# Decode attention with grouped queries: three zeroed tiles in one allocation with one memset, and the second and fourth K quarters of two tiles on shared semaphores

## Chip, cores and metric

One core of one Trainium2 chip. The metric is the device time of one execution in microseconds (us), lower is better. The record marks all executions told of here as fast, and all comparisons are between such runs. Engines: PE is TensorE (matmul), DVE is VectorE, ACT is ScalarE, POOL is GpSimd, SP is SyncE, which here only issues loads. "SPq" in a profile line is SP's instruction queue.

## Reference

```python
B, Hq, Hkv, Sq, Sk, D = 1, 32, 8, 1, 65536, 128      # all bf16
scores = einsum("bhqd,bhkd->bhqk", q, repeat(k, 4)) * D ** -0.5
out = einsum("bhqk,bhkd->bhqd", softmax(scores), repeat(v, 4))
```

K and V are 134 MB each and are read once. Each of the eight K/V heads serves four query rows.

## The kernel before

For each head g the keys are cut into two tiles (b = 0 and 1) of 32,768 keys, 8.39 MB each. SP issues the loads of K and V tiles in a fixed order into one big SBUF buffer with three slots: two for K, one for V.

```python
io = sb("io", [P, 3 * SL, D], bf16)        # three slots; SL = 256 rows of each partition
...
ex = sb("ex", [P, 4, 512], bf16)           # exponentials
et = sb("et", [P, 2, 512], bf16)
vs = sb("vs", [P, D + 2], fp32)            # sum of the value matmuls, and the two row sums
vy = sb("vy", [P, D, 4], fp32)
...
k_lo = [0, 64, 128, 192]
s_k = {(b, lo): sem(f"s_k{b}_{lo}") for b in range(2) for lo in k_lo}

def load_k(g, b):
    SP.wait((s_sc, 16 * g - 8 + 8 * b if g else 0))      # PE is done with the slot's old K
    cuts = k_lo + [SL] if (g, b) in ((0, 0), (G - 1, 1)) else [0, 128, SL] if g == 0 else [0, SL]
    for lo, hi in zip(cuts, cuts[1:]):
        load(k, g, b, 1 + b, s_k[b, lo], lo, hi)
...
load_k(0, 0)
load_k(0, 1)
for g in range(1, G):
    for b in range(2):
        load_k(g, b)
        load_v(g - 1, b)                                  # waits for PE to be done with the old V
```

DVE transposes each tile in four quarters, and before each it takes 16 from that quarter's semaphore. PE then computes scores in eight groups per tile and counts them in `s_sc`. The loop body is the same for every head, so all four quarters are always taken. But most tiles are loaded whole, and then only the first quarter's semaphore is paid by the load. The others are **prepaid**: POOL adds enough to them at a point where it can do no harm, and the later takes find the money there.

```python
def transposes(b, lo, hi):
    for t in range(lo, hi, 64):
        d_take(s_k[b, t], 16)                             # wait for 16, subtract 16
        part = io[:, (1 + b) * SL + t:(1 + b) * SL + t + 64, :]...
        dve.transpose(out=part, in_=part).then_inc(s_kt, 2)
```

POOL's start, before any of this, and DVE's:

```python
GP.mark(gp.memset(wz[:, :, :], 0.0))
GP.mark(gp.memset(vs[:, :], 0.0))
GP.mark(gp.memset(ex[:, :, :], 0.0))
GP.mark(gp.memset(vy[:, :, :], 0.0))
n = GP.mark(gp.memset(ident[:, :], 0.0))
GP.after(n)
p_ident = GP.mark(gp.affine_select(out=ident[:, :], ...))
...
for s in (s_k[1, 64], s_k[1, 192]):                       # prepaid from the start
    gp.sem_inc(s, 16 * (G - 1))
...
DV.mark(dve.memset(acc[:, :], 0.0))
DV.wait((s_gp, p_ident))
DV.mark(dve.tensor_reduce(out=sel[:, :], in_=ident..., op=ALU.add))
...                                                       # selq, sely, qT, y_sum, then the K transposes
```

## Time and profile before

| | before |
|---|---|
| median | 629.82 us (6 runs, 629.33 to 630.03) |
| span of the profiled execution | 627.7 us |
| busy: PE, DVE, ACT, POOL | 57%, 55%, 5%, 2% |
| transfers | 268.49 MB, mean 428 GB/s |

Three lines of the profile's page, before. The DMA row cuts the span into 40 slices; each digit is the busy share of the sixteen DMA engines in tenths.

```profile
PE   1865483827638275381844808458193571886346
DMA  8999999999999999999999999999999999999996
...
q1 hardware_dynamic: 6944, 268.45, 99.2%
```

PE comes and goes; the transfers never pause for a visible time. The queue that carries K and V fills 99.2% of the span.

The start, in the timeline of the kernel before. Columns: start in us, duration in us, engine, line, operation, output and input, count; in brackets, how long the engine had been idle and what released it.

```profile
1.52 0.21 POOL L187 MEMSET vs<- 128x130 f32 x1
1.67 1.81 POOL L188 MEMSET ex<- 128x2048 bf16 x1
3.41 0.52 POOL L189 MEMSET vy<- 128x512 f32 x1
...
4.65 0.38 DVE L208 TENSOR_REDUCE sel<-ident 128x4 f32<-128x128 f32 x1 [0.90 <-POOL ident L192]
...
8.50 4.45 DVE L373 STREAM_TRANSPOSE io<-io 128x4096 uint32<-128x4096 uint32 x1 [1.34 <-DVEq L119]
...
32.89 8.77 DVE L373 STREAM_TRANSPOSE io<-io 128x4096 uint32<-128x4096 uint32 x2 [5.11 <-DVEq L119]
```

DVE waits 0.90 us for POOL's identity. Later it waits again, 1.34 us, before its first K transpose, and there it waits for the first quarter of K to land, 7.4 us after its issue at 0.96 us (the release shows as DVE's own queue, in which the take of the load's semaphore stands). At 32.89 us the first half of K tile 1 has landed (issued at 2.97 us, 29.8 us to landing) and two quarters are transposed without a break.

The loads that SP issues next (timeline of SP, before):

```profile
33.28 0.43 SPq L137 DMA_DIRECT2D io<-in_v_dram  x1
57.31 0.33 SPq L137 DMA_DIRECT2D io<-in_k_dram  x1
95.12 0.33 SPq L137 DMA_DIRECT2D io<-in_v_dram  x1
```

And the end: three pieces of the chain of work that ended last, before (start, duration, what).

```profile
609.01 12.42 DMA io<-in_v_dram
...
622.53 1.80 PE pf L359 x28
...
624.89 0.36 ACT o L487
```

### The profile page before, as it was taken

The numbers are of one execution on the slowest core, as the hardware profiler recorded it, in microseconds if no ns is written. First come the engines' busy times: TensorE is split into PE (matmuls) and PEld (weight loads), VectorE is DVE, ScalarE is ACT, GpSimd is POOL, SyncE is SP. The second block draws the span as 40 slices with busy tenths as digits, with TensorE's granted clock in tenths as the row PEclk, the third lists the DMA queues.
The fourth block names the chain that finished last, engine by engine and source line by source line (L and its number), as shares of the span: only waits on it lengthen the run. The fifth ranks groups of instructions, "written<-read, shape, count | busy, mean of one in ns | idle before, by whom it ended". The sixth has DMA issues, their size and how long they took to land. (4 is left out here: it accounts for less than half of the span.)

```text
span 627.7 us, 7067 instructions
## 1 busy us (share of the span) xinstructions
PE 356.4 (57%) x2142; PEld 139.8 (22%) x2142; DVE 345.5 (55%) x154; ACT 34.4 (5%) x26; POOL 9.7 (2%) x42
## 2 busy tenths in 40 slices
PE   1865483827638275381844808458193571886346
PEld 0322131312213032130321303123031230332112
DVE  7795835649066490764807557084670946684210
ACT  0000100020000200002000020000200002000100
POOL 2000000000000000000000000000000000000000
PEclk9978595967959678596785958859587695899676
DMA  8999999999999999999999999999999999999996
GB/s 362 441 468 401 468 401 468 401 468 401 468 401 464 405 459 409 447 422 447 422 438 430 426 443 409 459 405 464 401 468 401 468 401 468 396 437 434 434 432 274
DMA packets 7003, 268.49 MB, mean 428 GB/s; under 512 B 856, under 2 KB 1112, under 8 KB 1496
## 3 DMA queue, kind: packets, MB, share of 16 engines
q1 hardware_dynamic: 6944, 268.45, 99.2%
q8 instruction: 1, 0.02, 0.0%
q14 instruction: 2, 0.02, 0.0%
q10 hardware_dynamic: 56, 0.01, 0.0%
HBM read 268.44 MB, written 0.01 MB: 428 GB/s over the span
## 5 line engine op out<-in xcount | busy, mean ns | idle before, releaser
L301 PE MATMUL acc<-io,wz 128*128 x1024 | 272.7, 420 | 184.8 <-PEq L119 157.3
L373 DVE STREAM_TRANSPOSE io<-io 128x4096 uint32<-128x4096 uint32 x64 | 279.9, 4416 | 157.2 <-DVEq L119 157.2
L301 PEld LDWEIGHTS acc<-io,wz 128*128 x1024 | 106.4, 104 | 351.2 <-issue 272.5
L254 PE MATMUL acc<-io,et 128*16 128x512 bf16 x1016 | 72.5, 416 | 19.3 <-PEq L119 19.2
L440 ACT ACTIVATE ex<-acc,nmb 128x2048 bf16<-128x2048 f32 x8 | 15.7, 1967 | 556.9 <-DVE nmb L420 556.9
L410 DVE TENSOR_REDUCE mg<-acc 128x1 f32<-128x2048 f32 x8 | 18.3, 2291 | 48.3 <-DVEq L119 48.3
L254 PEld LDWEIGHTS acc<-io,et 128*16 128x16 bf16 x1016 | 27.7, 94 | 58.4 <-issue 35.5
L248 PE MATMUL pf<-vs,sel 128*4 128x130 f32 (+1 forms) x20 | 5.7, 386 | 54.2 <-PEq L119 54.2
L376 DVE STREAM_TRANSPOSE et<-ex 128x1024 bf16<-128x1024 bf16 x17 | 20.8, 1225 | 22.6 <-SPq L154 12.8
L450 ACT ACTIVATE acc<-wz 128x2560 f32<-128x2560 bf16 (+2 forms) x8 | 16.3, 2040 | 1.0 <-ACT ex L440 0.2
L412 DVE TENSOR_REDUCE m<-pt 1x4 f32<-1x128 f32 x8 | 2.2, 279 | 22.7 <-DVEq L119 22.7
L514 POOL COPY wz<-qT 32x16 bf16<-32x16 bf16 x32 | 6.1, 189 | 512.6 <-PE acc L301 440.3
L248 PEld LDWEIGHTS pf<-vs,sel 128*4 128x4 f32 x20 | 1.2, 83 | 54.7 <-issue 54.6
L326 PE MATMUL pt<-et 128*16 128x512 bf16 x32 | 13.1, 411 | 0.0
L384 DVE TENSOR_REDUCE vs<-vy 128x128 f32<-128x512 f32 x9 | 6.1, 681 | 7.6 <-DVEq L119 7.6
L423 DVE TENSOR_TENSOR vy<-acc,sely 128x512 f32<-128x512 f32 x8 | 8.5, 1064 | 0.0
L472 DVE TENSOR_TENSOR vy<-acc,sely 128x512 f32<-128x512 f32 x1 | 0.7, 691 | 11.5 <-PE acc L254 11.5
L343 PE MATMUL pb<-ident,nrow 1*128 1x1 f32 x8 | 1.6, 194 | 7.5 <-PEq L119 7.5
L326 PEld LDWEIGHTS pt<-et 128*16 128x16 bf16 x32 | 3.1, 97 | 4.5 <-issue 1.4
L341 PE MATMUL pt<-ident,mg 128*1 128x128 f32 x8 | 2.3, 283 | 2.6 <-PEq L119 2.6
L420 DVE COPY nmb<-pb 128x1 f32<-128x1 f32 x8 | 1.3, 157 | 3.9 <-DVEq L119 3.9
L343 PEld LDWEIGHTS pb<-ident,nrow 1*128 1x128 f32 x8 | 1.1, 139 | 8.9 <-issue 8.9
(31 smaller groups left out, 22.8 us busy)
## 6 DMA issues: line engine op xcount, KB each, us to landing
io<-in_v_dram SPq DMA_DIRECT2D x5, 4096.0 KB, 16.9
io<-in_k_dram SPq DMA_DIRECT2D x8, 2048.0 KB, 27.4
io<-in_k_dram SPq DMA_DIRECT2D x2, 4096.0 KB, 34.4
io<-in_v_dram SPq DMA_DIRECT2D x1, 2048.0 KB, 10.3
io<-in_v_dram SPq DMA_DIRECT2D x1, 1024.0 KB, 12.4
io<-in_v_dram SPq DMA_DIRECT2D x3, 256.0 KB, 12.8
io<-in_v_dram SPq DMA_DIRECT2D x2, 128.0 KB, 12.8
io<-in_k_dram SPq DMA_DIRECT2D x13, 48.4
```

What stands on the lines that cost most here:

```text
L248: return pe.matmul(out=pf[0:H, 0:w], lhsT=sel[:, :], rhs=vs[:, 0:w], skip_group_check=True, **kw)
L254: return pe.matmul(out=vacc[32 * c:32 * c + 16, :, :], lhsT=et[:, ch // 2, w0:w0 + 16], rhs=io[:, PS * ch + 4 * tt:PS * ch + 4 * tt + 4, : ...
L301: i = pe.matmul(out=bass.AP(acc, r_o, [[2560, P], [1, 512]]), lhsT=bass.AP(wz, r_w + ((2 * s + e) * WB - 4 * u), [[4 * WB, P], [1, P]]), r ...
L326: pe.matmul(out=pt[0:16, :], lhsT=et[:, 0, 0:16], rhs=et[:, 0, :], start=True, stop=True)
L373: dve.transpose(out=part, in_=part).then_inc(s_kt, 2)
L376: dve.transpose(out=et[:, :, :].rearrange("p i n -> p (i n)"), in_=ex[:, 2 * b:2 * b + 2, :].rearrange("p i n -> p (i n)"),).then_inc(s_et, 1)
L384: DV.mark(dve.tensor_reduce(out=vs[:, 0:D], in_=vy[:, :, :], axis=AX.X, op=ALU.add))
L410: dve.tensor_reduce(out=mg[:, :], in_=sc, axis=AX.X, op=ALU.max).then_inc(s_mg, 1)
L423: dve.tensor_tensor(out=vy[:, :, :].rearrange("p d y -> p y d"), in0=vacc, in1=sely[:, :, None].to_broadcast([P, 4, D]), op=ALU.mult,).the ...
L440: act.activation(out=ex[:, :, :].rearrange("p b n -> p (b n)"), in_=sc, func=ACT.Exp, bias=nmb[:, :], scale=SCALE, accum_out=vs[:, D + g % ...
L450: act.activation(out=part, in_=wz[:, 0, 0:1].to_broadcast([P, part.shape[1]]), func=ACT.Copy).then_inc(s_cl, 1)
L514: gp.tensor_copy(out=wz[r, :, c0:c0 + H].rearrange("p (s w) h -> p s w h", s=2), in_=qTb[r, :, :, g, :],).then_inc(s_w, 1)
```

## The change

The intent: fewer POOL instructions and a shorter set-up, and two semaphores fewer in use. `ex`, `vy` and `vs` become views of one fp32 tile that one memset clears. For the second and fourth quarters, tile 1 now takes from tile 0's semaphore. Those can no longer be prepaid from the start, since tile 0's real quarters would be taken too early. POOL therefore waits for the eighth score group of tile 0 and pays fourteen takes then.

```diff
-    ex = sb("ex", [P, 4, 512], bf16)
     et = sb("et", [P, 2, 512], bf16)
-    vs = sb("vs", [P, D + 2], fp32)
-    vy = sb("vy", [P, D, 4], fp32)
+    zs = sb("zs", [P, 1024 + 4 * D + D + 2], fp32)
+    ex = zs[:, 0:1024].bitcast(bf16).rearrange("p (b n) -> p b n", n=512)
+    vy = zs[:, 1024:1024 + 4 * D].rearrange("p (d y) -> p d y", y=4)
+    vs = zs[:, 1024 + 4 * D:]
...
+    for lo in k_lo[1::2]:
+        s_k[1, lo] = s_k[0, lo]
...
-    GP.mark(gp.memset(vs[:, :], 0.0))
-    GP.mark(gp.memset(ex[:, :, :], 0.0))
-    GP.mark(gp.memset(vy[:, :, :], 0.0))
+    GP.mark(gp.memset(zs[:, :], 0.0))
...
-    for s in (s_k[1, 64], s_k[1, 192]):
-        gp.sem_inc(s, 16 * (G - 1))
...
+            if g == 1:
+                GP.wait((s_sc, 8))
+                for t in k_lo[1::2]:
+                    gp.sem_inc(s_k[0, t], 16 * (2 * G - 2))
             GP.wait((s_sc, 16 * g))
             gp.sem_inc(s_sd, 1)
             if g == 1:
-                for t in k_lo[1:]:
-                    gp.sem_inc(s_k[0, t], 16 * (G - 1))
+                gp.sem_inc(s_k[0, 128], 16 * (G - 1))
                 gp.sem_inc(s_k[1, 128], 16 * (G - 2))
```

## The prediction

> **What bounds the kernel now.** The transfers. The page's DMA row reads 9 tenths in all slices but the first and last; the queue table gives the K/V queue 99.2% of the sixteen engines' span, 268.45 MB at a mean of 428 GB/s. [...] PE is 57% busy, DVE 55%, POOL 2%. The chain of waits ends with the last V load and 6 us of tail (621.4 to 627.7 us), which the change doesn't touch.
>
> **What the change removes.** At the start, three POOL memsets (vs 0.207, ex 1.808, vy 0.524 us in the timeline; 2.36 us from start to start) become one over 1666 fp32 elements. Cost goes by elements, not bytes: 640 and 2048 bf16 took 0.631 and 1.808 us, 128 and 512 fp32 took 0.204 and 0.524 us; both give 0.10 us + 0.835 ns per element. ex cleared as fp32 has half the elements: estimate 0.10 + 1666 x 0.000835 = 1.49 us. POOL finishes the identity about 0.9 us earlier (4.62 to 3.7 us). DVE waits 0.9 us for it, but has its accumulator memset until 3.75 us, so its first reduction moves from 4.65 to about 3.8 us. Two early semaphore additions go too.
>
> **Where that lands.** DVE's set-up ends at about 6.3 instead of 7.17 us, but its first K transpose starts at 8.50 us because the first K quarter lands only then; DVE idles 1.34 us there now, 2.2 us after. The transfers start at 0.96 us on SP, which waits for none of this. Gain on the critical path: 0.
>
> **What the change adds.** At the first head the second and fourth quarters of K tile 1 may be taken only when POOL has seen eight score groups of tile 0 and paid the shared semaphores. PE ends those at 32.9 us. DVE waits until 32.89 us for the first half of tile 1 to land, transposes its first quarter for 4.4 us, and asks for the second at about 37.3 us. POOL is idle from 7.4 to 57.8 us, so it pays by about 33.3 us: 4 us of slack. The fourth quarter is asked for at about 47 us. From then on the shared semaphores hold 14 prepaid takes; the last K tile's real load is the sixteenth take. No new wait in steady state. A lost microsecond there would be hidden too: at 57.3 us, when DVE's and PE's progress releases the next K load, about 24 us of transfers are still queued.
>
> **SBUF.** The zeroed tiles move by a few KB; I expect the 1.2 us transposes, 1.97 us exponentials and 0.69 us sums unchanged.
>
> **Prediction.** 629.6 us, range 628.6 to 630.7; faster by over 2% 0.01, within 2% 0.98, slower by over 2% 0.01.
>
> **What would show it.** One POOL memset of 128x1666 fp32 near 1.49 us; DVE's first identity reduction at 3.8 us; its idle before the first K transpose 2.2 us, start still near 8.5 us; two transposes of tile 1 from 32.9 us unbroken (about 8.8 us); SP's loads at the old times within a microsecond; 428 GB/s and the same tail.
>
> **What would make it wrong.** The payment coming after 37.3 us, splitting tile 1's transposes; the memset colliding with DVE's set-up past 8.5 us; moved tiles slowing transposes or exponentials; a transfer rate that depends on something moved here. More than a microsecond would need the load queue to run dry, for which the trace gives no sign.

The forecast: about 0.9 us of POOL's set-up saved, 0 us of it on the critical path, so 629.6 us.

## The result, and the profile after

| | before | after |
|---|---|---|
| median, 6 runs each | 629.82 us (629.33 to 630.03) | 630.26 us (629.92 to 630.46) |
| span of the profiled execution | 627.7 us | 628.5 us |
| PE, DVE, ACT, POOL busy | 57, 55, 5, 2% | 56, 55, 5, 1% |

The ratio of the times is 1.0008 with a 95% interval of 0.9996 to 1.0021: the same. A ratio here is the mean time of one kernel's fast runs over the mean of the other's in the same rounds, so it isn't quite the ratio of the medians in the table.

The page after, the same rows:

```profile
PE   1865483827538185481844808458183572876436
DMA  8999999999999999999999999999999999999996
...
q1 hardware_dynamic: 6944, 268.45, 99.0%
```

The start, timeline of the changed kernel:

```profile
1.52 1.49 POOL L191 MEMSET zs<- 128x1666 f32 x1
...
3.73 0.38 DVE L208 TENSOR_REDUCE sel<-ident 128x4 f32<-128x128 f32 x1
...
8.29 4.45 DVE L373 STREAM_TRANSPOSE io<-io 128x4096 uint32<-128x4096 uint32 x1 [2.05 <-DVEq L121]
...
32.69 8.77 DVE L373 STREAM_TRANSPOSE io<-io 128x4096 uint32<-128x4096 uint32 x2 [5.11 <-DVEq L121]
```

The memset is as long as estimated, 1.49 us, and DVE's first reduction comes 0.92 us earlier. DVE then waits longer for the same thing, the first K quarter: 2.05 us instead of 1.34. The first quarter was 0.2 us earlier in this execution; the experiments below have 8.54, 8.46 and 8.44 us for it with and without the memset, so that is scatter. The pair at 32.69 us is unbroken, 8.77 us as before: the late payment isn't felt.

SP's loads after:

```profile
33.08 0.43 SPq L139 DMA_DIRECT2D io<-in_v_dram  x1
57.10 0.33 SPq L139 DMA_DIRECT2D io<-in_k_dram  x1
94.77 0.33 SPq L139 DMA_DIRECT2D io<-in_v_dram  x1
```

They are 0.2 to 0.35 us earlier. They buy nothing, because the queue still had work when they were issued: the last of the three took 24.9 us from issue to landing (24.8 before), and E8 will show 21.9 us for one on an empty queue. The end of the chain after:

```profile
608.53 12.98 DMA io<-in_v_dram
...
622.44 2.94 PE pf L359 x28
...
625.92 0.36 ACT o L487
```

The last V load on the chain lands at 621.51 us (608.53 + 12.98) against 621.43 before: the same. What differs is the tail: the 28 last value matmuls take 2.94 us, not 1.80. The stretch from 623 to 626 us shows why; first line before, second after. The columns are stretch, length, then busy us and instruction counts of PE, PE's weight loads, DVE, ACT and POOL, then the granted PE clock (1.00 is full), DMA share and GB/s.

```profile
623.00:626.00 3.00, 1.79 (x30) 1.47 (x26) 1.03 (x4) 0.36 (x1) 0.00 (x0) 1.00 0.10 26
```

```profile
623.00:626.00 3.00, 2.82 (x29) 2.59 (x27) 0.94 (x4) 0.08 (x1) 0.00 (x0) 0.64 0.08 23
```

The granted clock was 1.00 in one tail and 0.64 in the other. One such matmul took 219 ns (median) before and 314 ns after. In the clock records of these two traces (38 before, 40 after) every stretch stands at 0.50 or at 1.00, and 0.64 is a mean over both. They also say when it steps: before, it is 0.50 from 612.6 us and 1.00 from 622.8 us, just after the 28 matmuls begin; after, it is 1.00 from 618.4 us, 0.50 again from 621.8 us, and 1.00 only from 625.2 us. Which level meets the tail is the open question that the experiments had to take up: is it the change, or chance?

### The profile page after: what moved, and what is told of

Same layout as the page of the kernel before. It is cut to its first block, busy times and chain, and to the rows that moved or that the text cites. A ratio compares the mean times of both kernels' runs of the same rounds, so it can differ in the third digit from the quotient of the medians.

```text
span 628.5 us, 7063 instructions
## 1 busy us (share of the span) xinstructions
PE 351.4 (56%) x2142; PEld 139.2 (22%) x2142; DVE 345.5 (55%) x154; ACT 34.4 (5%) x26; POOL 8.8 (1%) x40
## 5 line engine op out<-in xcount | busy, mean ns | idle before, releaser
L301 PE MATMUL acc<-io,wz 128*128 x1024 | 268.4, 413 | 189.7 <-PEq L121 158.6
L301 PEld LDWEIGHTS acc<-io,wz 128*128 x1024 | 104.9, 102 | 353.3 <-issue 273.4
L254 PE MATMUL acc<-io,et 128*16 128x512 bf16 x1016 | 71.0, 410 | 21.3 <-PEq L121 20.1
L440 ACT ACTIVATE zs<-acc,nmb 128x2048 bf16<-128x2048 f32 x8 | 15.7, 1967 | 556.2 <-DVE nmb L420 556.2
L248 PE MATMUL pf<-zs,sel 128*4 128x130 f32 (+1 forms) x20 | 5.7, 387 | 53.3 <-PEq L121 53.3
L376 DVE STREAM_TRANSPOSE et<-zs 128x1024 bf16<-128x1024 bf16 x17 | 20.8, 1225 | 22.9 <-SPq L158 13.1
L384 DVE TENSOR_REDUCE zs<-zs 128x128 f32<-128x512 f32 x9 | 6.1, 681 | 7.6 <-DVEq L121 7.6
L423 DVE TENSOR_TENSOR zs<-acc,sely 128x512 f32<-128x512 f32 x8 | 8.5, 1065 | 0.0
L472 DVE TENSOR_TENSOR zs<-acc,sely 128x512 f32<-128x512 f32 x1 | 0.7, 691 | 11.9 <-PE acc L254 11.9
L359 PE MATMUL pf<-io,et 128*4 128x128 bf16 x32 | 3.5, 298 | 0.0
```

Of the source, the lines that this page charges most:

```text
L248: return pe.matmul(out=pf[0:H, 0:w], lhsT=sel[:, :], rhs=vs[:, 0:w], skip_group_check=True, **kw)
L254: return pe.matmul(out=vacc[32 * c:32 * c + 16, :, :], lhsT=et[:, ch // 2, w0:w0 + 16], rhs=io[:, PS * ch + 4 * tt:PS * ch + 4 * tt + 4, : ...
L301: i = pe.matmul(out=bass.AP(acc, r_o, [[2560, P], [1, 512]]), lhsT=bass.AP(wz, r_w + ((2 * s + e) * WB - 4 * u), [[4 * WB, P], [1, P]]), r ...
L359: i = pe.matmul(out=fin, lhsT=et[:, 1, w0:w0 + H], rhs=io[:, t, :], start=(t == SL - TAIL), stop=(t == SL - 1), skip_group_check=True,)
L376: dve.transpose(out=et[:, :, :].rearrange("p i n -> p (i n)"), in_=ex[:, 2 * b:2 * b + 2, :].rearrange("p i n -> p (i n)"),).then_inc(s_et, 1)
L384: DV.mark(dve.tensor_reduce(out=vs[:, 0:D], in_=vy[:, :, :], axis=AX.X, op=ALU.add))
```

## Experiments

Theory A: the kernel is bound by its load queue. Set-up and payment both have slack, so neither part of the change reaches the end. Rival B: DVE's set-up and waits lie on the path; the memset gained about 0.9 us, and the new wait gave it back. Rival C: the 0.4 us between the medians is real and comes from the moved tiles.

### E1 to E3: the halves alone, and the whole again (same chip, five rounds)

E1 is the kernel before with only the allocation and the memset of the diff; E2 has only the semaphore part; E3 is the changed kernel again.

```diff
 E1:  - ex, vs, vy and their three memsets   + zs, its views, one memset     (semaphores as before)
 E2:  + s_k[1, lo] = s_k[0, lo], payment after the wait for s_sc 8           (tiles as before)
```

> Only the first part of the change: one allocation, one memset; the semaphores as before. Theory A (transfers bound the kernel, DVE's set-up has slack): the first identity reduction on DVE starts at 3.7 to 3.8 us instead of 4.65, the first K transpose stays within 0.3 us of 8.3 to 8.5 us, and the time is 629.8 us within 0.5 us, ratio 0.9993 to 1.0010. Rival B (set-up is on the critical path; the change gained about 0.9 us here and gave it back in the new semaphore wait): 0.6 to 1.0 us faster than before, ratio 0.9985. Rival C (the moved tiles cost something, and that is the 0.4 us by which the changed kernel looked slower): 0.3 to 0.6 us slower, with all of it here.

> Only the second part: the shared semaphores, with the three memsets and allocations as before. Theory A: the two first transposes of K tile 1 stay an unbroken pair of 8.8 us near 32.8 us, and the time is 629.8 us within 0.5 us. Rival B: 0.6 to 1.3 us slower than before, and the pair of transposes split by a wait. Rival C: no difference from before.

> The changed kernel once more, beside the two halves on the same chip. Theory A: 629.5 to 630.5 us, within 0.15% of before, so that the 0.4 us seen first is noise or a matter of the clock granted in the tail. Rival C: 0.3 to 0.6 us slower than before again, equal to the memset half. Rival B: equal to before by cancellation of the two halves.

| | median | ratio to before (95%) | first identity reduction | first K transpose |
|---|---|---|---|---|
| before, 9 runs | 629.77 us (629.20 to 630.60) | | 4.65 us | 8.50 us |
| E1 memset only | 629.60 us | 0.9996 (0.9983 to 1.0010) | 3.72 us | 8.54 us |
| E2 semaphores only | 629.51 us | 0.9998 (0.9985 to 1.0012) | 4.65 us | 8.44 us |
| E3 both | 629.68 us | 0.9996 (0.9983 to 1.0010) | 3.73 us | 8.46 us |

(The two times of the kernel before are from its own trace.) E1 shows the whole gain of the set-up and none in the time, and in E2 the pair of transposes stays whole (8.77 us at 32.80 us), so no new wait gave anything back. By itself E1's interval still allows a gain of up to 1.1 us; its trace speaks against it (the last V load on the chain lands at 621.52 us, 621.43 before), and E6 below excludes B. And E3 isn't slower than before: C's 0.4 us doesn't come back, though the intervals of E1 and E3 would still allow 0.6 us. In E3's tail the 28 matmuls took 1.82 us, at a granted clock of 1.00 from 623 to 626 us: the same kernel as the 2.94 us above. E3's line for that stretch:

```profile
623.00:626.00 3.00, 1.81 (x30) 1.50 (x27) 1.06 (x4) 0.36 (x1) 0.00 (x0) 1.00 0.07 20
```

The kernel before itself spread from 629.2 to 630.6 us here. So the clock in the tail is worth about 1.1 us and comes and goes with the same program. All nine traces here whose chain ends with the 28 matmuls in one piece agree: where the clock steps up 0.3 us after the first of them (before, E3), they take 1.80 and 1.82 us; 2.7 to 2.8 us after (after, E5), 2.94 and 2.96 us. The others lie at these ends or between: E1 1.82 us, with 219 ns as the median of one such matmul, as before; E9 1.79 us; E4, E6 and E7 2.52, 2.67 and 2.73 us, with medians of 314, 311 and 311 ns. In E2, E10 and E11 the last 12 matmuls waited for the last piece of V and took 0.83 us; in E2 none of that line took over 219 ns. Why the step falls where it does isn't settled; no run here controls it.

### E4 and E5: is it the load queue that bounds? (three rounds)

A load is cut short on purpose in one K tile in the middle; all engines still do all their work on whatever lies in the slot.

```diff
         cuts = k_lo + [SL] if ... else [0, SL]
+        if (g, b) == (3, 0):
+            cuts = [0, SL // 2]            # E4;  E5: [0, 3 * SL // 4]
```

> A wrong result on purpose: the changed kernel, but of one K tile in the middle (head 3, first half of the keys) only the first half of its rows is loaded, 4.19 MB less; all engines do the same work on what lies there. Theory A: at 427 to 434 GB/s that is 9.7 to 9.8 us of transfers, and the whole of it comes off: about 620.5 us. If the engines bound the kernel: no change, 630 us. In between would mean that the transfers have slack somewhere before the end.

E4: 622.47 us, ratio 0.9881 (0.9866 to 0.9896). 7.3 us came off, not 9.7. (The comparison with the reference passed, so it can't tell half a tile of one head; the kernel is wrong all the same.) An engine-bound kernel would have gained nothing, so the queue is the bound, but my sum missed something. The trace shows it. SP's next load after the short tile, and its time from issue to landing (the last column of the DMA view), first E4:

```profile
206.59 0.33 SPq L139 DMA_DIRECT2D io<-in_v_dram  x1
```

```profile
io<-in_v_dram SPq DMA_DIRECT2D x1, 21.8
```

The same load in E3, issued at the same point:

```profile
io<-in_v_dram SPq DMA_DIRECT2D x1, 29.4
```

A tile moves in about 19.4 us (8.39 MB at the 433 GB/s of E4's DMA view from 165 to 205 us; the K load right behind the V load above lands 19.4 us after it in E4). In E3 the load lands 29.4 us after its issue because other transfers were still before it. In E4 the queue had all but emptied: 21.8 us is what a tile takes alone, about 2.4 us more than the 19.4 us of its bytes. The short tile lands 38.9 us after its issue at about 168.1 us, so at 207.0 us; the next lands at 206.6 + 21.8 = 228.4 us. Between them lie 21.4 us, 2.0 more than a tile needs: the queue ran dry (E4's DMA view from 206 to 208 us shows no packet starting before 207.5 us, 0.9 us after the V load's issue). The tail's clock took about another 0.7 us (2.52 us for the 28 matmuls against E3's 1.82); together these are the missing 2.4 us within the scatter between executions.

That gives a measure that I should have read in the first place: **the lead of a load is its time from issue to landing, less the 21.9 us that a tile takes on an empty queue** (21.8 us in E4, 21.9 us in E8). In steady state it is 29.4 - 21.9 = 7.5 us.

> Wrong result on purpose, to find where 2.4 us of the half tile's 9.7 went. Theory A2 (the loads are issued about 10 us ahead of need, by the landing times, less about 2 us of latency; a tile shortened by 9.7 us lets the queue run dry just before the next issue): shortened by a quarter, 2.10 MB or 4.85 us, the queue doesn't run dry, and all of it comes off: 624.9 us, within 0.6 us. The next V load should land about 24.6 us after its issue, not 29.4. Rival (a fixed share of a transfer's saving is lost, as in the half tile, where 75% came off): 626.1 us.

For the "about 2 us of latency" E4 shows 2.4 us (21.8 less 19.4).

E5: 625.67 us, ratio 0.9937 (0.9920 to 0.9953), 3.8 us less than before by the medians, and just outside the 624.3 to 625.5 us expected. The next V load landed 24.6 us after its issue, as expected:

```profile
io<-in_v_dram SPq DMA_DIRECT2D x1, 24.6
```

And the last load of the chain landed at 616.77 us against 621.45 in E3, 4.7 us earlier. But the tail met the slow clock:

```profile
603.75 13.02 DMA io<-in_v_dram
...
617.86 2.96 PE pf L361 x28
```

2.96 us against 1.82 returned 1.1 us of it. So, in the execution that was profiled, the queue no longer ran dry and the transfers gave nearly the whole saving, 4.7 of 4.85 us; the time by itself would have spoken for the rival.

### E6 and E7: how much delay does the set-up bear? (three rounds)

The large memset is repeated on POOL, each repeat waiting for the last.

```diff
-    GP.mark(gp.memset(zs[:, :], 0.0))
+    for _ in range(4):                     # E6;  E7: range(10)
+        GP.after(GP.mark(gp.memset(zs[:, :], 0.0)))
```

> The changed kernel with its large memset done four times, each waiting for the last: DVE's set-up ends about 5 us later, the first K transpose starts at about 11.7 us, 3.2 us late. Theory A: the load of K for the second head is still issued, at about 36.3 us, before the first two tiles have landed (42.3 us), so no change of the time: 629.8 us within 0.5 us. Rival B (set-up is on the critical path): 3.2 us slower, 633 us.

E6: 629.76 us, ratio 1.0000 (0.9983 to 1.0017). The first identity reduction came at 8.47 us and the first K transpose at 10.90 us, 2.4 us late, and all of it vanished. Rival B's shift of 3.2 us, or of the 2.4 us that it came to, didn't appear and lies outside the interval.

> The memset done ten times: the first K transpose at about 22 us, 13.6 us late. Theory A: the load of K for the second head is issued at about 46.7 us, after the queue has run dry near 41 us, and lands about 21.5 us later, 68.2 us against 61.7: 6.4 us are lost and never made good, 636 us (634.3 to 637.3). Rival B: the whole 13.6 us, 643 us. If the set-up had no way to the end at all: 629.8 us.

E7: 636.16 us, ratio 1.0103 (1.0086 to 1.0120). Its timeline:

```profile
17.74 0.38 DVE L209 TENSOR_REDUCE sel<-ident 128x4 f32<-128x128 f32 x1 [13.99 <-POOL ident L195]
...
20.17 17.41 DVE L374 STREAM_TRANSPOSE io<-io 128x4096 uint32<-128x4096 uint32 x4
```

The total fell where it was expected, but partly by luck. The repeats cost less than I had put down, so DVE was 11.7 us late, not 13.6, and so was the K load that this releases (the V load right behind it went out at 44.94 us, 33.23 in E3). Its lead in the unchanged kernel is 28.9 - 21.9 = 7.0 us; 11.7 us of delay less 7.0 makes 4.7. (The K load landed 21.8 us after its issue, where 21.5 us was the estimate.) The last V load on the chain landed 5.9 us later (627.37 against 621.45 us), and the tail's 28 matmuls took 2.73 us, 0.9 more than in E3. The trace places the difference between 4.7 and 5.9. The delayed K load lands 4.6 us later than its like in E3 (it goes out 11.7 us later, and takes 21.8 us instead of 28.9), but the V load issued at 102.93 us, instead of 95.08, lands 6.1 us later, 23.0 us after its issue. That is the load that E8 will show to have the smallest lead, and the sum of issue and 21.9 us falls 1.1 us short there. So the sums with the lead are good to about a microsecond. What the two runs show together: a delay of the set-up was free while it stayed within the lead of 7.0 us of the load that it releases (2.4 us in E6), and what went beyond was paid (in E7 an expected 4.7 us, 5.9 us at the last V load on the chain).

### E8 to E10: how much delay does the payment bear? (three rounds)

Small memsets on a scratch tile stand between POOL's wait and its payment.

```diff
                 GP.wait((s_sc, 8))
+                for _ in range(60):        # E8;  E9: 12;  E10: 30
+                    GP.after(GP.mark(gp.memset(scr[:, :], 0)))     # 128 x 384 uint8
                 for t in k_lo[1::2]:
                     gp.sem_inc(s_k[0, t], 16 * (2 * G - 2))
```

> The changed kernel with about 40 us of idle memsets on POOL between its wait for the eighth score group and the payment of the shared semaphores: payment at about 72.6 us, DVE asks for it at 37.1 us and waits 35 us; the load of K released by the sixteenth group is issued at about 92.6 us, not 57.1, when the queue has been dry since about 80 us. Theory A: the 35.5 us of waiting costs only what the queue doesn't cover: 13.7 us, 643.5 us (641 to 646). Rival B: all of it, 665 us.

E8: 650.86 us, ratio 1.0334 (1.0316 to 1.0351). A miss, twice over. The dose was smaller than meant: a memset with its wait came every 0.474 us, so POOL paid at 61.3 us and DVE waited 24 us, not 35. And the price was higher: 21 us, not 13.7. E8's DVE:

```profile
61.50 4.45 DVE L374 STREAM_TRANSPOSE io<-io 128x4096 uint32<-128x4096 uint32 x1 [24.26 <-DVEq L122]
```

Its SP, and the time from issue to landing of the second of these loads:

```profile
81.50 0.33 SPq L140 DMA_DIRECT2D io<-in_k_dram  x1
119.31 0.33 SPq L140 DMA_DIRECT2D io<-in_v_dram  x1
```

```profile
io<-in_v_dram SPq DMA_DIRECT2D x1, 21.9
```

The K load of 57 us has a lead of 43.2 - 21.9 = 21.3 us (43.2 us from issue to landing in the kernel before). On that one alone, a delay of 24.4 us would have cost 3.1. But the chain of work shifts as a whole, and the V load that went out at 94.8 to 95.1 us goes out at 119.3. Its lead in the kernel before:

```profile
io<-in_v_dram SPq DMA_DIRECT2D x1, 24.8
```

24.8 - 21.9 = 2.9 us, the smallest that I found. 24.4 less 2.9 is 21.5 us: what was measured. I had looked at the load that the delayed step releases next, not at the tightest one behind it. E9 and E10 were made to test this reading with doses on both sides of 2.9 us.

> 12 idle memsets on POOL before the payment, at the 0.474 us each that the run with 60 showed: payment at about 38.6 us, DVE asks at 37.2 us and waits about 1.4 us, so the pair of transposes of K tile 1 is split. Theory A3 (the tightest load is not the one issued at 57.1 us but the V load at 94.8 us, which lands 24.7 us after its issue where an empty queue takes 21.9 us: a lead of 2.8 us): everything after moves by 1.4 us, the V load is issued at about 96.2 us, and the time doesn't change: 629.7 us within 0.6 us. Rival B (each microsecond of DVE's wait counts): 631.1 us.

> 30 idle memsets: payment at about 47.1 us, DVE waits 9.9 us. Theory A3: the V load is issued 9.9 us late at 104.7 us, of which 2.8 us are covered: 7.1 us lost, 636.8 us (635.8 to 637.8), with the V load landing 21.9 us after issue. My earlier reading (the load of 57.1 us is the tightest, covered by 21 us): 629.7 us. Rival B: 639.6 us.

E9: 630.08 us, ratio 1.0008 (0.9992 to 1.0025). E10: 636.50 us, ratio 1.0113 (1.0096 to 1.0129). E9's DVE and SP:

```profile
38.56 4.45 DVE L374 STREAM_TRANSPOSE io<-io 128x4096 uint32<-128x4096 uint32 x1 [1.48 <-DVEq L122]
```

```profile
96.22 0.33 SPq L140 DMA_DIRECT2D io<-in_v_dram  x1
```

E10's:

```profile
47.20 4.45 DVE L374 STREAM_TRANSPOSE io<-io 128x4096 uint32<-128x4096 uint32 x1 [9.99 <-DVEq L122]
```

```profile
104.85 0.33 SPq L140 DMA_DIRECT2D io<-in_v_dram  x1
```

Even with the pair of transposes split by 1.48 us, E9 loses nothing that can be told from noise. (Its interval alone would leave room for the whole 1.4 us; but in its trace the last V load on the chain lands at 621.88 us, only 0.4 us after E3's.) In E10 the wait was 9.99 us, and the time rose by 7.0 us over the kernel before's 629.47 us in the same rounds: 9.99 less 2.9 is 7.1. Both other readings (nothing, or all of it) miss by 3 us or more. The V load landed 22.2 us after its issue (21.9 expected), and the queue did stand still before it. The stretch from 100 to 105.75 us, first E10, then E9; the last two columns are DMA share and GB/s:

```profile
100.00:105.75 5.75, 4.77 (x71) 1.87 (x69) 5.22 (x2) 0.00 (x0) 0.00 (x0) 1.00 0.00 0
```

```profile
100.00:105.75 5.75, 0.00 (x0) 0.00 (x1) 5.16 (x2) 0.00 (x0) 0.00 (x0) 0.57 0.92 399
```

The added memsets don't visibly slow DVE: its transpose beside them takes 4.45 us in E9 (at 32.63 us), as elsewhere.

E9 also places the payment of the changed kernel itself: its first delaying memset starts at 32.72 us, just when POOL's wait is met. So the plain payment falls a little after 32.7 us, some 4 us before DVE asks (37.1 us).

### E11: by elements or by bytes? (three rounds)

```diff
-    GP.mark(gp.memset(zs[:, :], 0.0))
+    GP.mark(gp.memset(zs[:, :].bitcast(bf16), 0.0))
```

> The changed kernel with its one memset written as 3332 bf16 elements over the same bytes. If the cost goes by elements, 0.10 us + 3332 x 0.000835 = 2.88 us, not 1.49, the identity comes 1.4 us later and DVE's first reduction starts at about 5.1 us; its first K transpose stays at 8.3 to 8.5 us and the time at 629.7 us within 0.6 us. If the cost goes by bytes, 1.49 us again.

E11: 629.84 us, ratio 1.0010 (0.9993 to 1.0027). Its timeline:

```profile
1.52 2.88 POOL L191 MEMSET zs<- 128x3332 bf16 x1
...
5.11 0.38 DVE L208 TENSOR_REDUCE sel<-ident 128x4 f32<-128x128 f32 x1 [1.36 <-POOL ident L194]
```

The same bytes as bf16 took 2.88 us against 1.49: the cost goes by elements. The scratch memsets of E8 (384 uint8 elements, 0.417 us each) lie on the same line, 0.10 us + 0.835 ns per element. So most of what the memset half of the change saves comes from clearing `ex` as half as many, wider elements; one instruction instead of three saves at most the 0.10 us of each of two starts.

## Why the prediction was right, point by point

- **The bound.** Right. The DMA row and the 99% were read rightly; E4 and E5 confirm it by taking bytes away: an estimated 9.7 and 4.85 us of transfers less, 7.3 and 3.8 us off the time.
- **The memset.** Right: 1.49 us predicted and measured, first reduction predicted at 3.8 us, 3.73 measured.
- **Its gain on the path, zero.** Right, shown by E6 (2.4 us of delay, no time) and, within its noise, by E1 (all of the gain, no time).
- **The payment and its 4 us of slack.** Right: the pair is unbroken after, and E9 places the payment at 32.7 us.
- **"A lost microsecond there would be hidden too."** True for a microsecond or two (E9), but the reason given was incomplete. The sum named the load of 57.3 us with "about 24 us of transfers still queued". The tightest load behind the step is the V load at 95 us, with 2.9 us of lead. The prediction never used the 24 us as a limit, but E8's expectation did, and missed by 7 us (by 18 us with the dose that it got: 3.1 against 21.4); E10 shows the true limit.
- **The moved tiles.** No cost seen: E1 ratio 0.9996 (up to 1.0010); transposes of `ex` 1.20 us, exponentials 1.97 us, `vs` sums 0.69 us as before.
- **"The same tail."** Not in the execution that was profiled: 1.1 us longer at a granted clock of 0.64. E3 shows the fast tail with the same program. That may be the 0.4 us between the first medians, which the interval of the ratio doesn't tell from zero; only one of those six executions after has a trace here, so for the other five it is not shown.

## What to carry to other kernels

Here, with one load queue busy for 99% of the span, an edit in set-up or synchronisation was worth nothing until it moved an issue by more than that load's lead (E9: 1.48 us of wait, no time that could be told; E10: 9.99 us of wait against 2.9 us of lead, 7.0 us). In a kernel whose profile looks like this, read each load's lead as its time from issue to landing less what the same load takes on an empty queue, and take the smallest of all the loads behind the edited step, not the next one. Here that told the price of a delay to about a microsecond. Differences of a microsecond at the end of such a kernel should be looked for in the last matmuls and their granted clock before they are put down to the edit (here 1.82 against 2.94 us with the same program). POOL cleared the same bytes as fp32 in about half the time of bf16 (1.49 against 2.88 us, E11); that shortens the set-up, and here it was worth nothing in the time.
